# Seven half products for eight in the first layer of eleven pairs

## The chip, the cores and the metric

The kernel runs on one core of a Trainium2 chip. The metric is the device time of one execution in microseconds. Times are the median of three runs; one further execution was recorded by the hardware profiler.

## The reference

Attention with a decay (32 heads of 576 positions, head size 64) gives 2304 tokens of width 512. Two layers of the same shape follow, all in fp32:

```
x = attention(q, k, v, f)                 # 2304 x 512
h = x @ w_in;  g = relu(h)**2             # w_in: 512 x 2048
x = g @ w_out                             # w_out: 2048 x 512
h = x @ w_in2                             # second set of weights, same shapes
g = where(h >= 1, h, where(h <= -1, 0, (h + 1)**2 / 4))
out = g @ w_out2
```

Every fp32 operand of a matmul is kept as a high part (fp32r) and a low part, and each product is three matmuls: high by high, high by low, low by high.

## The kernel before

Tokens are kept as columns, in four blocks: three of 512 and a last one of 768 (`HALF` is 384). Blocks one to three run through each of the two layers pair by pair of steps: step `s` is one slice of 128 hidden units. `h_group` (L1119) makes its first layer with 12 matmuls, `act_group` (L1137) the activation and its two parts, `out_group` (L1167) adds 12 matmuls to four PSUM banks, two steps later (`LAG`). The weights of a step lie in a buffer `whl` of the ring `big` (L464, six buffers), loaded from the copy `scr` in DRAM by `w_load` (L1004). In it lie the first layer's slice of step `s + LAG` and the second layer's of step `s`. The attention of the block that follows is spread over both passes of a block: that of block three over block two, that of the last over block three. Each of its tasks sends its probabilities through transposing transfers (L930) before PE multiplies them with v (L954).

The last block is `last_block` (L1255). For each of the two layers' sets (`mo` 0 and 1, called the first and the second half here), eight pairs `c` of slices run in a first phase. A pair's first layer is four results (slice `j` by token half `k`), each 12 matmuls of 384 columns (L1333) in a PSUM bank of kind `h`; the ring `ps` has four banks, of which two hold the sums `b` (L471). ACT and DVE apply the activation and write a slot of `G` (L1344 to L1357). The second layer is done with seven half products per pair for eight already: `split` (L1274) makes high and low parts of a slot or a difference of slots, and `product` (L1287) adds 2 x 3 matmuls to two banks, which makes one half product. Three of a pair's products (`a`, `c`, `b`) stand in the first phase; the other four run in two later phases. The sums of w_out that they need are made by `weight_sums` (L1233) during the first phase: two adds 512 wide, four adds or differences 256 wide, then high and low part of each half. The first half goes to the products at once (`sum`), the other to DRAM (`scr2`), for the phase after.

Two loads bring a pair's weights from DRAM: `wi`, 1 MB in two transfers, and `wo`, the same, each into one `big` buffer. All transfers but one are issued from SP's queue.

Every operation is handed to a planner (`Schedule`, L153 on) with a due time, its costs on the engines that may do it, its dependencies and its buffers. The planner picks engine and order; the order of each engine is then fixed in the program. Rings marked fifo give their buffers out in the order in which they are made.

Of the kernel before, what the change touches and what calls it, by code (L numbers as in the profile page):

```python
# [22 lines left out]
P = 128  # L23
# [4 lines left out]
LAG = 2  # L28
# [366 lines left out]
HALF = WIDTH[LAST] // 2  # L395
NPAIR = NFC // 2
EARLY = 2


@with_exitstack  # L400
def tile_attention_moe_moe(ctx: ExitStack, tc: tile.TileContext, qkv, f, w2, outT):
# [831 lines left out]
    def weight_sums(i, due, W, o_w):  # L1233
# [18 lines left out]
        sum_op[i] = load(due + 12, lambda: Wf.tile, lambda: scr2[i], P * 4096, done[1:], [Wf], 2.0)  # L1252
        return Sb, done[0]

    def last_block():  # L1255

        n, A, v = HALF, nc.scalar, nc.vector
        x, x2 = xb[LAST], None
        t_h, t_p = 12 * mm_t(n), 6 * mm_t(n)
        t_a = 4 * t_h + 3 * t_p  # L1260
        span_mo = NPAIR * (4 * t_h + 7 * t_p)
        x2_ops = {}

        for mo in range(2):
            T0 = V[NS] + 4 * mm_t(512) + mo * span_mo
# [37 lines left out]
                return [last[key, i] for i in range(2)]  # L1303

            for c in range(NPAIR):
                tA = T0 + c * t_a
                nm = f"{mo}_{c}"
                W0, W1 = new("big", f"wi{nm}"), new("big", f"wo{nm}")
                o_w0, i = [], mo * NPAIR + c
                for j in range(2):  # L1310
                    pr = mo * NFC + (2 * c + j - LAG) % NFC
                    o_w0.append(load(tA - 8, lambda pr=pr: scr[pr][:, 0], lambda W0=W0, j=j: W0.tile[:, j].bitcast(F32),
                                     P * 4096, [scr_op[pr, 0]], [W0]))
# [5 lines left out]
                Sb, o_sb = weight_sums(i, tA, W1, o_w1)  # L1319
                gb = new("G", f"G{nm}")  # L1320
                G.append(gb)
                slots = {(0, 0): 0, (0, 1): 1, (1, 0): 2, (1, 1): 3}
                order = [(j, k) for k in (range(2) if mo == 0 else (1, 0)) for j in range(2)]
                src = x if mo == 0 else x2
                og = {}
                for at, (j, k) in enumerate(order):
                    t0 = tA + at * t_h
                    ps = new("ps", f"h{nm}_{j}{k}", kind="h")
                    o = None
                    for kc in range(NKC):  # L1330
# [12 lines left out]
                    if mo == 0:
# [16 lines left out]
                slot = lambda q, gb=gb: (lambda: gb.tile[:, q, :])  # L1360
                sp1 = split(f"1_{nm}", tA + t_h + 1.5, gb, 0, [og[0, 0]], True)
# [13 lines left out]
            tB = T0 + NPAIR * t_a + 2  # L1375
# [49 lines left out]
            for q in range(NPAIR // 2):  # L1425
                t0 = tB + 4 * q * t_p
                sb = new("big", f"s34_{mo}_{q}", [P, 2, 2, 2, 256])
                for j in range(2):
                    c = 2 * q + j
                    o_l = load(t0 - 7, lambda q=mo * NPAIR + c: scr2[q], lambda sb=sb, j=j: sb.tile[:, j].bitcast(F32),  # L1430
                               P * 4096, [sum_op[mo * NPAIR + c]], [sb])
# [122 lines left out]
```

## Time and profile before

| | us |
|---|---|
| three runs | 923.92, 925.12, 925.60 |
| median | 925.12 |
| profiled execution | 924.2 |
| its span, first to last instruction | 922.4 |
| PE busy | 913.6 |
| DVE busy | 750.7 |
| ACT busy | 688.6 |

The span has these stages: attention of block one up to about 30 us, blocks one to three up to 661, the last block's first half up to about 796 (its first phase ends near 759), and its second half to the end. PE is busy nearly throughout. The granted clock of PE is 0.999 of full speed. A busy time is the time that instructions were recorded, from first start to last end; the records of two instructions of one engine can overlap.

### The profile page before, as it was taken

The numbers are of one execution on the slowest core, as the hardware profiler recorded it, in microseconds if no ns is written. First come the engines' busy times: TensorE is split into PE (matmuls) and PEld (weight loads), VectorE is DVE, ScalarE is ACT, GpSimd is POOL, SyncE is SP. The second block draws the span as 40 slices with busy tenths as digits, with TensorE's granted clock in tenths as the row PEclk, the third lists the DMA queues.
The fourth block names the chain that finished last, engine by engine and source line by source line (L and its number), as shares of the span: only waits on it lengthen the run. The fifth ranks groups of instructions, "written<-read, shape, count | busy, mean of one in ns | idle before, by whom it ended". The sixth has DMA issues, their size and how long they took to land.

```text
span 922.4 us, 14271 instructions
## 1 busy us (share of the span) xinstructions
PE 913.6 (99%) x4674; PEld 798.8 (87%) x4674; DVE 750.7 (81%) x1738; ACT 688.6 (75%) x1375; POOL 30.6 (3%) x129
## 2 busy tenths in 40 slices
PE   8999999999999999999999999999999999999998
PEld 7678888887888888888888888888899999999998
DVE  8999999999868788887677778888677647899774
ACT  7998988999877787888778777886556555646553
POOL 4010001000000000000000000000000000000000
PEclk9999999999999999999999999999999999999999
DMA  8799999998998886989798897986687657676562
GB/s 230 246 355 399 353 402 323 363 344 323 329 297 254 249 281 205 329 226 278 234 290 278 270 267 210 277 224 179 203 289 267 222 197 279 238 264 229 213 228 86
DMA packets 132954, 247.38 MB, mean 268 GB/s; under 512 B 90513, under 2 KB 92721, under 8 KB 118097
## 3 DMA queue, kind: packets, MB, share of 16 engines
q1 hardware_dynamic: 132872, 246.47, 81.8%
q8 instruction: 37, 0.61, 0.3%
q14 instruction: 37, 0.29, 0.1%
q10 hardware_dynamic: 8, 0.00, 0.0%
HBM read 178.62 MB, written 46.84 MB: 244 GB/s over the span
## 4 chain that ended last, share of the span: by engine, by line
PE 90%; DVE 5%; ACT 2%; DMA 1%; POOL 1%; issue 1%; DVEq 0%; POOLq 0%; ACTq 0%
PE h L1129 27%; PE h L1333 13%; PE acc L1180 9%; PE acc L1182 9%; PE acc L1181 9%; PE av L954 4%; PE s L847 2%; PE s L848 2%; PE b L1296 2%; PE b L1298 2%; PE b L1297 2%; PE c L1296 1%; PE c L1298 1%; PE c L1297 1%; PE a L1297 1%; PE a L1298 1%
## 5 line engine op out<-in xcount | busy, mean ns | idle before, releaser
L1129 PE MATMUL h<-x,whl 128*128 128x512 f32 x1128 | 284.1, 393 | 0.0
L1129 PEld LDWEIGHTS h<-x,whl 128*128 128x128 f32 x1128 | 209.6, 188 | 42.5 <-issue 0.5
L1180 PE MATMUL acc<-gh,whl 128*128 128x512 f32 x384 | 150.6, 392 | 0.0
L1182 PE MATMUL acc<-gl,whl 128*128 128x512 f32 x384 | 150.1, 391 | 0.0
L1181 PE MATMUL acc<-gh,whl 128*128 128x512 f32 x384 | 149.9, 390 | 0.0
L1182 PEld LDWEIGHTS acc<-gl,whl 128*128 128x128 f32 x384 | 72.0, 188 | 15.6
L1180 PEld LDWEIGHTS acc<-gh,whl 128*128 128x128 f32 x384 | 72.1, 188 | 14.5 <-issue 0.9
L1181 PEld LDWEIGHTS acc<-gh,whl 128*128 128x128 f32 x384 | 72.1, 188 | 13.8
L881 ACT ACTIVATE E<-E,st 64x320 f32<-64x320 f32 (+2 forms) x96 | 63.4, 661 | 24.8 <-DVE st L642 19.5
L635 DVE TENSOR_TENSOR gl<-g,gh 128x512 fp32r<-128x512 f32 x96 | 65.9, 686 | 16.5 <-PE acc L1182 10.7
L642 DVE CUSTOM_DVE_ANT_0 E<-s,mask 128x288 f32<-128x288 f32 (+2 forms) x128 | 59.8, 500 | 20.6 <-PE s L848 20.2
L923 DVE SCALAR_TENSOR_TENSOR PP<-E,st,PP 128x512 f16<-128x512 f32 (+2 forms) x128 | 69.9, 592 | 5.2 <-ACT PP L919 4.3
L1333 PE MATMUL h<-x,wi 128*128 128x384 f32 x384 | 71.9, 334 | 0.0
L1333 PE MATMUL h<-x_last,wi 128*128 128x384 f32 x384 | 71.1, 336 | 0.2 <-DVE G L1357 0.2
L919 ACT ACTIVATE PP<-E,st 128x512 f16<-128x512 f32 (+2 forms) x128 | 66.9, 590 | 5.9 <-DVE st L893 4.5
L1333 PEld LDWEIGHTS h<-x_last,wi 128*128 128x128 f32 x384 | 66.8, 188 | 1.1 <-DVE G L1357 0.7
L1333 PEld LDWEIGHTS h<-x,wi 128*128 128x128 f32 x384 | 67.1, 188 | 0.4
L1227 DVE TENSOR_TENSOR G<-G 128x384 f32<-128x384 f32 x64 | 34.4, 554 | 18.7 <-ACT G L1349 18.0
L626 DVE CAST pr<-PT 128x640 fp32r<-128x640 f16 (+2 forms) x88 | 31.2, 405 | 21.7 <-DMA PT<-PP 21.7
L1160 DVE SCALAR_TENSOR_TENSOR g<-r,h 128x512 f32<-128x512 f32 x48 | 32.8, 683 | 15.5 <-ACT r L1158 14.9
L623 ACT ACTIVATE pr<-PT 128x640 fp32r<-128x640 f16 (+2 forms) x72 | 37.9, 580 | 10.0 <-DMA PT<-PP 8.8
L1156 ACT ACTIVATE r<-h,half 128x512 f32<-128x512 f32 x48 | 32.6, 679 | 16.1 <-PE h L1129 16.0
(340 smaller groups left out, 1791.6 us busy)
## 6 DMA issues: line engine op xcount, KB each, us to landing
whl<-scr SPq DMA_DIRECT2D x56, 1024.0 KB
raw<-in_w_dram SPq DMA_DIRECT2D x28, 1024.0 KB
scr<-whl SPq DMA_DIRECT2D x28, 1024.0 KB
wo<-scr SPq DMA_DIRECT2D x48, 512.0 KB
in<-in_qkv_dram SPq DMA_DIRECT2D x32, 608.0 KB
wi<-scr SPq DMA_DIRECT2D x32, 512.0 KB
whl<-scr SPq DMA_DIRECT2D x16, 512.0 KB
sum<-wfs SPq DMA_DIRECT2D x16, 512.0 KB
```

The lines of the kernel that those rows point to most:

```text
L623: alts["ACT"] = (act_t(n, psum), lambda: nc.scalar.activation(out(), in_(), AF.Copy))
L635: alts["DVE"] = (dve_t(n), lambda: nc.vector.tensor_sub(out(), a(), b()), True)
L642: return nc.vector.tensor_tensor_reduce(out=out, in0=ps, in1=mask[:m, OFF - q0:OFF - q0 + n], scale=scale, scalar=3e38, op0=ALU.add, op1=A ...
L881: nc.scalar.activation(Ec.tile[:m, :e], Ec.tile[:m, :e], AF.Exp, scale=-1.0, bias=nmx(), accum_out=st.tile[:m, 1, ci:ci + 1])))}, [*tops, ...
L919: nc.scalar.activation(hi, x, AF.Copy, scale=r())
L923: nc.vector.scalar_tensor_tensor(lo, x, r(), hi, op0=ALU.mult, op1=ALU.subtract)
L954: nc.tensor.matmul(av.tile[:, c0:W], vt.tile[:, kc, :, :], dst()[:, i, :], start=(j == 0), stop=(j == len(parts) - 1))
L1129: nc.tensor.matmul(ps.tile[:, :n], w.tile[:, 0, wi, kc * P:(kc + 1) * P], src.tile[:, kc, xi, :n], start=(kc == 0 and i == 0), stop=(kc == ...
L1180: nc.tensor.matmul(a.tile[:, :n], wh, gh.tile[:, :n], start=(fc == 0), stop=False)
L1181: nc.tensor.matmul(a.tile[:, :n], wl, gh.tile[:, :n], start=False, stop=False)
L1182: nc.tensor.matmul(a.tile[:, :n], wh, gl.tile[:, :n], start=False, stop=(fc == NFC - 1))
L1333: nc.tensor.matmul(ps.tile[:, :n], W0.tile[:, j, wi, kc * P:(kc + 1) * P], src.tile[:, kc, xi, k * n:(k + 1) * n], start=(kc == 0 and i == ...
```

## The change

In the last block, pairs 2 to 7 of the first half and 3 to 7 of the second (`SEVEN`) make their first layer with seven half products of six matmuls each, on two PSUM banks, in place of four results of 12. The function `seven` does it. It needs sums of w_in (four per pair) and sums of the tokens. The token sums are made once per half by `token_sums`, on DVE and ACT, due while pair 0 runs; their parts are kept in `xa` and in buffers of `o` and `g`, which the last block doesn't use otherwise at that time. The sums of w_in are made in block three by `pair_sums`, in the pass over the same weights, from the `whl` buffers of two steps, and stored in DRAM (`scr3`, high and low part, 0.5 MB each); `seven` loads them into a third `big` buffer per pair. Of `wi` such a pair loads only three of four quarters.

For pairs 3 to 6 of the second half (`OUTS`) the sums of w_out come the same way from block two (`scr4`); for these `weight_sums` is not called.

The core of the diff:

```diff
+SEVEN = ((2, 3, 4, 5, 6, 7), (3, 4, 5, 6, 7))
+SUMS_AT = (2, 2)
+OUTS = ((), ((1, 3), (1, 4), (1, 5), (1, 6)))
...
+    def in_sums(s):
+        blk, mo, fc = steps[s]
+        c = fc // 2
+        if fc % 2 == 0:
+            if blk == SUMS_AT[mo] and c in SEVEN[mo]:
+                pair_sums(s, s - LAG, 0, scr3[mo, c], in_sum_op)
+            if (blk, c) in OUTS[mo]:
+                pair_sums(s, s, 1, scr4[mo, c], out_sum_op)
+
+    def pair_sums(s, first, layer, store, ops):
...
+        due = V[s + 1] + 2 * layer
+        Wf, Sf, Sh = new("wf", f"wfi{nm}"), new("low", f"si{nm}", [P, 4, 256], F32), new("wf", f"shi{nm}")
+        for j in range(2):
+            w, o_w = whl[first + j], whl_op[first + j]
+            o_f.append(add(due + j, lambda j=j: Wf.tile[:, j], lambda w=w: w.tile[:, layer, 0].bitcast(F32),
+                           lambda w=w: w.tile[:, layer, 1].bitcast(F32), 512, o_w, [w, Wf]))
...
+        o1 = add(due + 2, S[0], A21, A22, 256, o_f[1:], [Wf, Sf])
+        o2 = add(due + 2.5, S[1], S[0], A11, 256, [o1, o_f[0]], [Wf, Sf], sub=True)
+        o3 = add(due + 3, S[2], A11, A21, 256, o_f, [Wf, Sf], sub=True)
+        o4 = add(due + 3.5, S[3], A12, S[1], 256, [o2], [Wf, Sf], sub=True)
+        o5 = sch.op(due + 4, copies(lambda: flat(Sh), src, 1024, "ACT DVE"), [o3, o4], [Sf, Sh])
+        o6 = sch.op(due + 5, subs(lambda: flat(Wf), src, lambda: flat(Sh).bitcast(F32), 1024, "DVE"), [o5], [Sf, Sh, Wf])
+        ops[mo, c] = [load(due + 10 + i, ..., P * 4096, [o], [b], 2.0) for i, b, o in ((0, Sh, o5), (1, Wf, o6))]
...
+        def token_sums(due, mo, x, x_ops):
...
+            for kk in range(2):
+                xf, tf = new("G", f"xf{mo}{kk}"), new("G", f"tf{mo}{kk}")
+                o_x = [add(due + kk * 6, lambda q=q, whole=whole: whole(q), lambda q=q, kk=kk: x.tile[:, 2 * q + kk, 0].bitcast(F32),
+                           lambda q=q, kk=kk: x.tile[:, 2 * q + kk, 1].bitcast(F32), 2 * n, x_ops(2 * q + kk), [x, xf])
+                       for q in range(2)]
+                o1 = add(due + kk * 6 + 1, T[0], B12, B11, n, o_x[:1], [xf, tf], sub=True)
+                o2 = add(due + kk * 6 + 1.5, T[1], B22, T[0], n, [o1, o_x[1]], [xf, tf], sub=True)
+                o3 = add(due + kk * 6 + 2, T[2], B22, B12, n, o_x, [xf, tf], sub=True)
+                o4 = add(due + kk * 6 + 2.5, T[3], B21, T[1], n, [o2], [xf, tf], sub=True)
+                for t, o in enumerate((o1, o2, o3, o4)):
+                    o = sch.op(due + kk * 6 + 3, copies(hi, T[t], n, "ACT DVE"), [o], [tf, hb])
+                    o = sch.op(due + kk * 6 + 4, subs(lo, T[t], lambda hi=hi: hi().bitcast(F32), n, "DVE"), [o], [tf, hb, lb])
+
+        def seven(mo, c, tA, W0, o_w0, gb, x, x_ops):
+            sb = new("big", f"si{nm}")
+            o_s = [load(tA - 6, ... scr3[mo, c][:, i] ..., P * 4096, [in_sum_op[mo, c][i]], [sb]) for i in range(2)]
+            X, Y = (new("ps", f"{z}{nm}", kind="h") for z in "XY")
+            c_ = [new("C", f"c{i}{nm}") for i in range(3)]
+            p, q, v_ = ((lambda b=b: b.tile) for b in c_)
...
+            m1 = mul(0, X, A_(0, 0), B_(0, 0), True, [], c_)
+            o_p = sch.op(tA + t_p, copies(p, xs, n, "ACT DVE", psum=True), [m1], [X, c_[0]])
+            m6 = mul(1, Y, S_(1), T_(1), True, [])
+            o_q = plus(2, q, ys, p, [m6, o_p], [Y, c_[0], c_[1]])
+            m2 = mul(2, X, A_(0, 1), B_(1, 0), False, [m1, o_p])
+            g11 = act(3, xs, 0, m2, X, True)
+            m7 = mul(3, Y, S_(2), T_(2), False, [m6, o_q])
+            o_v = plus(4, v_, ys, p, [m7, o_p], [Y, c_[0], c_[2]])
+            m5 = mul(4, X, S_(0), T_(0), True, [m2, g11])
+            o_22 = plus(5, v_, xs, v_, [m5, o_v], [X, c_[2]])
+            m4 = mul(5, Y, A_(1, 1), T_(3), False, [m7, o_v])
+            o_21 = plus(6, p, ys, p, [m4, o_q, o_v], [Y, c_[0]])
+            m3 = mul(6, X, S_(3), B_(1, 1), False, [m5, o_22])
+            o_12 = plus(7, q, xs, q, [m3, o_q], [X, c_[1]])
+            return {(0, 0): g11, (1, 1): act(5.5, v_, 3, o_22, c_[2]), (1, 0): act(6.5, p, 2, o_21, c_[0]),
+                    (0, 1): act(7.5, q, 1, o_12, c_[1])}
...
+                    z = 256 if c in SEVEN[mo] and j else 0
+                    o_w0.append(load(tA - 8, ... scr[pr][:, 0, :, z:] ..., P * 8 * (512 - z), [scr_op[pr, 0]], [W0]))
...
+                if (mo, c) in scr4:
+                    Sb = new("sum", f"sum{nm}")
+                    o_sb = load(tA + t_a - 7 * t_p, ... scr4[mo, c][:, :, :2] ..., P * 4096, out_sum_op[mo, c], [Sb])
+                else:
+                    Sb, o_sb = weight_sums(i, tA, W1, o_w1)
...
+                if c in SEVEN[mo]:
+                    og = seven(mo, c, tA, W0, o_w0, gb, src, x_ops)
+                if c == 0 and SEVEN[mo]:
+                    token_sums(tA + 4, mo, src, x_ops)
-                for at, (j, k) in enumerate(order):
+                for at, (j, k) in enumerate(() if og else order):
...
             w_decode(s + 1)
+            in_sums(s)
```

In `act`, the first result (`g11`) is read from its bank; where the second half's activation or the first half's `g11` needs it, ACT writes `r` first. The other three results are read from SBUF.

## Rows read from the trace of the kernel before

**Rows 1.** The page: part 1, then the first line of part 4.

```profile
PE 913.6 (99%) x4674; PEld 798.8 (87%) x4674; DVE 750.7 (81%) x1738; ACT 688.6 (75%) x1375; POOL 30.6 (3%) x129
...
PE 90%; DVE 5%; ACT 2%; DMA 1%; POOL 1%; issue 1%; DVEq 0%; POOLq 0%; ACTq 0%
```

**Rows 2.** Busy times by stretch; the first row names the columns.

```profile
core 0: us, PE busy (x) PEld busy (x) DVE busy (x) ACT busy (x) POOL busy (x), PEclk, DMA share, GB/s
30.00:140.00 110.00, 109.93 (x538) 87.42 (x537) 108.44 (x203) 101.23 (x179) 7.51 (x3) 1.00 0.96 358
350.00:455.00 105.00, 105.00 (x512) 89.01 (x511) 87.37 (x232) 83.01 (x174) 1.76 (x19) 1.00 0.83 253
455.00:555.00 100.00, 100.00 (x489) 84.74 (x488) 74.68 (x203) 78.85 (x170) 2.20 (x24) 1.00 0.88 269
555.00:660.00 105.00, 104.86 (x504) 88.31 (x503) 84.69 (x211) 78.55 (x162) 1.87 (x18) 1.00 0.82 224
685.00:708.00 23.00, 23.00 (x135) 23.00 (x134) 16.50 (x33) 13.02 (x26) 0.00 (x0) 1.00 0.89 299
812.00:830.00 18.00, 17.80 (x102) 17.48 (x102) 17.10 (x36) 9.65 (x18) 0.00 (x0) 1.00 0.72 259
830.00:853.00 23.00, 23.00 (x134) 22.78 (x133) 21.09 (x42) 14.14 (x26) 0.00 (x0) 1.00 0.64 229
```

**Rows 3.** Timeline of PE, 690 to 730: start, us, engine, line, operation, tiles, count.

```profile
704.45 3.80 PE L1333 MATMUL h<-x,wi 128*128 128x384 f32 x21
...
715.89 3.80 PE L1333 MATMUL h<-x,wi 128*128 128x384 f32 x21
```

**Rows 4.** Timeline of all engines, 880 to 890: two banks handed over; [idle before <-releaser].

```profile
881.89 0.33 PE L1298 MATMUL a<-gl,wo 128*128 128x384 f32 x1
...
882.28 1.00 ACT L623 ACTIVATE p<-a 128x384 f32<-128x384 f32 x2
...
882.81 0.19 PEld L1296 LDWEIGHTS a<-ghaB,wo 128*128 128x128 f32 x1 [0.39 <-ACT p L623]
...
885.35 0.33 PE L1298 MATMUL c<-ghl,sum 128*128 128x384 f32 x1
...
885.72 1.08 DVE L1227 TENSOR_TENSOR w<-c,p 128x384 f32<-128x384 f32 x2
...
886.33 0.19 PEld L1296 LDWEIGHTS c<-ghlcB,s 128*128 128x128 f32 x1 [0.45 <-DVE w L1227]
```

**Rows 5.** Timeline of DVE, 700 to 730, the same columns.

```profile
699.93 0.42 DVE L1227 TENSOR_TENSOR sf<-wfs 128x256 f32<-128x256 f32 x1
700.39 0.42 DVE L1227 TENSOR_TENSOR sf<-sf,wfs 128x256 f32<-128x256 f32 x1
...
702.80 0.69 DVE L635 TENSOR_TENSOR wfs<-sf,wfs 128x512 fp32r<-128x512 f32 x1
703.41 0.55 DVE L635 TENSOR_TENSOR gl<-G,gh 128x384 fp32r<-128x384 f32 x1
...
713.66 1.02 DVE L1227 TENSOR_TENSOR G<-G 128x384 f32<-128x384 f32 x2
```

**Rows 6.** Timelines, one activation in each half: ACT from 705.69, all from 800.22.

```profile
705.69 0.49 ACT L1344 ACTIVATE r<-h 128x384 f32<-128x384 f32 x1 [0.41 <-PE h L1333]
706.22 0.53 ACT L1349 ACTIVATE G<-r 128x384 f32<-128x384 f32 x1
...
800.22 0.58 ACT L1352 ACTIVATE r<-h,half 128x384 f32<-128x384 f32 x1 [1.94 <-PE h L1333]
...
801.39 0.55 DVE L1357 SCALAR_TENSOR_TENSOR G<-r,h 128x384 f32<-128x384 f32 x1 [2.20 <-ACT r L1354]
```

**Rows 7.** SP's own waits, 662 to 760: who waited for whom, us, times, longest.

```profile
SPq L1223 <- PE a L1298: 51.2, 9, 9.5
```

**Rows 8.** Waits of all engines, 447 to 661, the same columns.

```profile
DVE pr L626 <- DMA PT<-PP: 11.9, 10, 1.9
```

More of the change, by code (lines that the diff above doesn't have):

```diff
@@ L1253, in weight_sums @@
         return Sb, done[0]
+    scr3 = {(mo, c): dram.tile([P, 2, 4, 256], F32, name=f"in_sum{mo}_{c}") for mo in range(2) for c in SEVEN[mo]}
+    scr4 = {(mo, c): dram.tile([P, 2, 4, 256], F32, name=f"out_sum{mo}_{c}") for mo in range(2) for _, c in OUTS[mo]}
+    in_sum_op, out_sum_op = {}, {}
+    def in_sums(s):
[7 more added lines that the diff above has]
+    def pair_sums(s, first, layer, store, ops):
+        blk, mo, fc = steps[s]
+        c = fc // 2
+        nm = f"{layer}_{mo}_{c}"
+        due = V[s + 1] + 2 * layer
+        Wf, Sf, Sh = new("wf", f"wfi{nm}"), new("low", f"si{nm}", [P, 4, 256], F32), new("wf", f"shi{nm}")
+        o_f = []
+        for j in range(2):
+            w, o_w = whl[first + j], whl_op[first + j]
+            o_f.append(add(due + j, lambda j=j: Wf.tile[:, j], lambda w=w: w.tile[:, layer, 0].bitcast(F32),
+                           lambda w=w: w.tile[:, layer, 1].bitcast(F32), 512, o_w, [w, Wf]))
+        (A11, A12), (A21, A22) = ([lambda j=j, z=z: Wf.tile[:, j, z:z + 256] for z in (0, 256)] for j in range(2))
+        if layer:
+            A12, A21 = A21, A12
+        S = [lambda i=i: Sf.tile[:, i] for i in range(4)]
+        o1 = add(due + 2, S[0], A21, A22, 256, o_f[1:], [Wf, Sf])
+        o2 = add(due + 2.5, S[1], S[0], A11, 256, [o1, o_f[0]], [Wf, Sf], sub=True)
+        o3 = add(due + 3, S[2], A11, A21, 256, o_f, [Wf, Sf], sub=True)
+        o4 = add(due + 3.5, S[3], A12, S[1], 256, [o2], [Wf, Sf], sub=True)
+        src = lambda: Sf.tile.rearrange("p a n -> p (a n)")
+        flat = lambda b: b.tile.rearrange("p a n -> p (a n)").bitcast(F32R)
+        o5 = sch.op(due + 4, copies(lambda: flat(Sh), src, 1024, "ACT DVE"), [o3, o4], [Sf, Sh])
+        o6 = sch.op(due + 5, subs(lambda: flat(Wf), src, lambda: flat(Sh).bitcast(F32), 1024, "DVE"), [o5], [Sf, Sh, Wf])
+        ops[mo, c] = [load(due + 10 + i, lambda b=b: b.tile.rearrange("p a n -> p (a n)"),
+                             lambda i=i: store[:, i].rearrange("p a n -> p (a n)"), P * 4096, [o], [b], 2.0)
+                        for i, b, o in ((0, Sh, o5), (1, Wf, o6))]
     def last_block():
@@ new lines, in seven, with A_, S_, B_ @@
+        def seven(mo, c, tA, W0, o_w0, gb, x, x_ops):
+            nm = f"7{mo}_{c}"
+            sb = new("big", f"si{nm}")
+            o_s = [load(tA - 6, lambda i=i: scr3[mo, c][:, i].rearrange("p a n -> p (a n)"),
+                        lambda i=i: sb.tile[:, i].rearrange("p a n -> p (a n)").bitcast(F32), P * 4096, [in_sum_op[mo, c][i]], [sb])
+                   for i in range(2)]
+            X, Y = (new("ps", f"{z}{nm}", kind="h") for z in "XY")
+            c_ = [new("C", f"c{i}{nm}") for i in range(3)]
+            p, q, v_ = ((lambda b=b: b.tile) for b in c_)
+            xs, ys = lambda: X.tile[:, :n], lambda: Y.tile[:, :n]
+            def A_(j, k):
+                return W0, [o_w0[j]], lambda i, kk: W0.tile[:, j, i, 256 * k + P * kk:256 * k + P * kk + P]
+            def S_(i):
+                return sb, o_s, lambda h, kk: sb.tile[:, h, i // 2, 256 * (i % 2) + P * kk:256 * (i % 2) + P * kk + P]
+            def B_(k, t):
+                return [x], [o for kk in range(2) for o in x_ops(2 * k + kk)], lambda i, kk: x.tile[:, 2 * k + kk, i, t * n:(t + 1) * n]
+            def T_(t):
+                return ([b for kk in range(2) for b in tsum[mo, t, kk][1]], [tsum[mo, t, kk][2] for kk in range(2)],
+                        lambda i, kk: tsum[mo, t, kk][0][i]())
+            def mul(at, bank, a, b, start, deps, extra=()):
+                (wb, wo, wt), (bs, bo, bt) = a, b
+                def mms():
+                    todo = [(kk, wi, xi) for kk in range(2) for wi, xi in ((0, 0), (0, 1), (1, 0))]
+                    for z, (kk, wi, xi) in enumerate(todo):
+                        nc.tensor.matmul(bank.tile[:, :n], wt(wi, kk), bt(xi, kk), start=start and z == 0,
+                                         stop=z == len(todo) - 1, skip_group_check=not start)
+                return sch.op(tA + at * t_p, {"PE": (6 * mm_t(n), mms)}, [*deps, *wo, *bo],
+                              list(dict.fromkeys([bank, wb, *bs, *extra])), mlp=True)
+            plus = lambda at, out, a, b, deps, bufs: add(tA + at * t_p, out, a, b, n, deps, bufs, psum=True)
+            def act(at, src, slot, dep, buf, bank=False):
+                out, due = lambda: gb.tile[:, slot, :], tA + at * t_p
+                r = None if mo == 0 and not bank else new("r", f"r{nm}_{slot}")
+                rt = lambda: r.tile[:, :n]
+                def on_act():
+                    A.activation(src(), src(), AF.Relu)
+                    A.activation(out(), src(), AF.Square)
+                port = () if bank else (True,)
+                if r is None:
+                    return sch.op(due, {
+                        "DVE": (dve_t(n), lambda: v.scalar_tensor_tensor(out(), src(), 0.0, src(), op0=ALU.max, op1=ALU.mult), True),
+                        "ACT": (2 * act_t(n), on_act)}, [dep], [buf, gb])
+                if mo == 0:
+                    o = sch.op(due, {"ACT": (act_t(n, True), lambda: A.activation(rt(), src(), AF.Relu))}, [dep], [buf, r])
+                    return sch.op(due + 0.5, {
+                        "DVE": (dve_t(n), lambda: v.scalar_tensor_tensor(out(), src(), 0.0, rt(), op0=ALU.max, op1=ALU.mult)),
+                        "ACT": (act_t(n), lambda: A.activation(out(), rt(), AF.Square))}, [o], [buf, r, gb])
+                def squared():
+                    A.activation(rt(), src(), AF.Relu, scale=0.5, bias=half)
+                    A.activation(rt(), rt(), AF.Square)
+                o = sch.op(due, {"ACT": (act_t(n, True, 1) + act_t(n), squared)}, [dep], [buf, r])
+                return sch.op(due + 1, {"DVE": (dve_t(n), lambda: v.scalar_tensor_tensor(
+                    out(), rt(), 1.0, src(), op0=ALU.min, op1=ALU.max), *port)}, [o], [buf, r, gb])
+            m1 = mul(0, X, A_(0, 0), B_(0, 0), True, [], c_)
[14 more added lines that the diff above has]
+                    (0, 1): act(7.5, q, 1, o_12, c_[1])}
@@ L1305, in last_block @@
             for c in range(NPAIR):
-                tA = T0 + c * t_a
+                tA = T0 + starts[mo][c]
                 nm = f"{mo}_{c}"
@@ L1311, in last_block @@
                     pr = mo * NFC + (2 * c + j - LAG) % NFC
[L1312 to L1313 removed]
+                    z = 256 if c in SEVEN[mo] and j else 0
+                    o_w0.append(load(tA - 8, lambda pr=pr, z=z: scr[pr][:, 0, :, z:], lambda W0=W0, j=j, z=z: W0.tile[:, j, :, z:].bitcast(F32),
+                                     P * 8 * (512 - z), [scr_op[pr, 0]], [W0]))
                 o_w1 = []
@@ L1318, in last_block @@
                                      P * 4096, [scr_op[pr, 1]], [W1]))
-                Sb, o_sb = weight_sums(i, tA, W1, o_w1)
+                if (mo, c) in scr4:
+                    Sb = new("sum", f"sum{nm}")
+                    o_sb = load(tA + t_a - 7 * t_p, lambda c=c: scr4[mo, c][:, :, :2].rearrange("p t a n -> p t (a n)"),
+                                lambda Sb=Sb: Sb.tile.bitcast(F32), P * 4096, out_sum_op[mo, c], [Sb])
+                else:
+                    Sb, o_sb = weight_sums(i, tA, W1, o_w1)
                 gb = new("G", f"G{nm}")
@@ L1325, in last_block @@
                 og = {}
-                for at, (j, k) in enumerate(order):
+                x_ops = lambda kc: xops[LAST, kc] if mo == 0 else [x2_ops[kc, k] for k in range(2)]
+                if c in SEVEN[mo]:
[3 more added lines that the diff above has]
+                for at, (j, k) in enumerate(() if og else order):
                     t0 = tA + at * t_h
@@ L1360, in last_block @@
                 slot = lambda q, gb=gb: (lambda: gb.tile[:, q, :])
+                te -= t_p * (c in SEVEN[mo])
                 sp1 = split(f"1_{nm}", tA + t_h + 1.5, gb, 0, [og[0, 0]], True)
@@ L1374, in last_block @@
                              [o_sb], sp6, first, stop)
-            tB = T0 + NPAIR * t_a + 2
+            tB = T0 + starts[mo][NPAIR] + 2
             o_u, o_w = [], []
@@ L1429, in last_block @@
                     c = 2 * q + j
-                    o_l = load(t0 - 7, lambda q=mo * NPAIR + c: scr2[q], lambda sb=sb, j=j: sb.tile[:, j].bitcast(F32),
-                               P * 4096, [sum_op[mo * NPAIR + c]], [sb])
+                    done = (mo, c) in scr4
+                    part = scr4[mo, c][:, :, 2:].rearrange("p t a n -> p t (a n)") if done else scr2[mo * NPAIR + c]
+                    o_l = load(t0 - 7, lambda part=part: part, lambda sb=sb, j=j: sb.tile[:, j].rearrange("p t a n -> p t (a n)").bitcast(F32),
+                               P * 4096, out_sum_op[mo, c] if done else [sum_op[mo * NPAIR + c]], [sb])
                     for z, key, slot, dep, e in ((1, "c", 3, "b22", 0), (0, "b", 1, "t3", 1)):
```

16 lines of the change are left out of this document (15 added, 1 removed).

## The prediction

> **What bounds the kernel now.** I read the page first: TensorE (PE) is busy 913.6 of 922.4 us, and 90% of the chain that ended last is PE [rows 1]. That is an average, so next comes the table of stretches, where the reader should look at the PE and the VectorE (DVE) columns side by side [rows 2]. PE is full nearly throughout: 105.00 of 105.00 us in block two's second pass, 100.00 of 100 and 104.86 of 105 in block three, 23.00 of 23.00 in the last block's first half. The largest share that it misses in these rows is 0.20 us of the 18 from 812 to 830, where DVE is at 17.10. So in the last block a PE instruction taken away is worth its own time, as long as nothing else reaches 100%. DVE is the candidate: 16.50 of 23 us in the first half of the last block, 21.09 of 23 in the second, 75 to 83% in blocks two and three. What a busy DVE can do without stopping PE is seen from 30 to 140 us: DVE 108.44 of 110, and PE 109.93.
>
> **What is removed.** Now a pair's first layer is eight half products of six matmuls, and its second layer adds three more in the first phase. The timeline of PE gives the step of one matmul: 21 take 3.80 us, the last one shown to its end, so (3.80 - 0.33)/20 = 0.1735 us [rows 3, 4]; a half product is 6 x 0.1735 = 1.04 us, and 11 of them are 11.44, which is also the distance from one pair to the next (715.89 - 704.45) [rows 3]. Eleven pairs lose one half product each: 11 x 1.04 = 11.4 us of PE that is on the path. Such a pair then lasts 10.40 us.
>
> Four pairs of the second half also lose their weight sums: two adds 512 wide, four 256 wide, two differences 512 wide. By starts in the timeline of DVE, 512 wide is 0.61 us (702.80 to 703.41), 256 wide behind its own result 0.46 (699.93 to 700.39), 384 wide 0.47 (two in 1.02, one taking 0.55) [rows 5]: 4 x 0.61 + 4 x 0.46 = 4.3 us of DVE a pair. PE gets nothing from that directly; it pays for what follows.
>
> **What is added in the last block.** A seven-product pair runs on two PSUM banks in turn. Each product waits until the bank's last product has been dealt with, and one other product (1.04 us) lies between. Five of these steps are adds on DVE from PSUM that are not there today. I price them by the add of the same kind that exists, w<-c,p, two in 1.08 us, so 0.47 to 0.55 each [rows 4]: 5 x 0.47 = 2.35 us. The pair's DVE work in the first half is then 4.3 (weight sums) + 4 x 0.47 (G adds) + 3 x 0.47 (splits) + 2.35 = 9.9 us of 10.40; in the second half four activations come on top and, in four of the five pairs, the weight sums go: 4 x 0.47 + 3.3 + 2.35 = 7.5. DVE fits, barely in the first half. ACT gets one copy more a pair and the squares of g11, some 0.5 to 1 us, and has 13.02 of 23 us in use [rows 2].
>
> Does the hand-over fit under the 1.04 us? One place shows it bare, where a phase of the last block ends: the last matmul into a starts at 881.89, ACT copies at 882.28, the next matmul into that bank loads at 882.81, after 0.39 us of idle; by DVE 885.35, 885.72, 886.33, with 0.45 idle [rows 4]. From the last matmul's start that is 0.92 and 0.98 us, so 0.75 and 0.81 after it is issued: 0.23 to 0.29 us to spare, if the engine is free at that moment. One step is longer. The first result of each pair is squared straight from its bank. In the first half that is two ACT steps, 0.53 apart, the second 0.53 long [rows 6]: 0.39 + 1.06 + 0.04 - 0.17 = 1.32 after issue, 0.28 too long. In the second half it is two ACT steps and one on DVE, 801.39 + 0.55 - 800.22 = 1.72 [rows 6], which makes 0.39 + 1.72 + 0.06 - 0.17 = 2.00, 0.96 too long. Over six and five pairs: 6 x 0.28 + 5 x 0.96 = 6.5 us at most, and 0 at least, since each pair has three second-layer products (3.12 us) that wait for none of this and can stand there. I take a quarter, **1.6**, as one uncovered wait of today (0.39 less the 0.17 of a matmul) is about a quarter of 0.96.
>
> The other six hand-overs of a pair, 66 in all, cost nothing if DVE is free, and up to 0.47 - 0.23 = 0.24 us each behind another add: 0 to 15.8, the far end being a DVE that never is free (A, below). I take **1.0**, near zero, because from 812 to 830 a DVE at 95% took only 0.20 us from PE in 18 [rows 2].
>
> Token sums: once in each half, 4 adds 768 wide (no row; between one and two 384-wide ones, I take 2 x 0.47), 8 differences and 8 low parts at 0.47: 11.3 us of DVE, while pairs 0 and 1 (first half) or 0 to 2 (second) still run the old way. Old pairs need 4.3 + 3.3 = 7.6 there and 9.5 here, so 26.5 us fall due in 22.9 and 39.8 in 34.3: a debt of 3.6 and 5.5. Later pairs pay back 6 x 0.5 = 3.0 and 4 x 2.9. Cost 0 to 9.1; I take **1.7**: the unpaid 0.6 of the first half and a fifth of the second's.
>
> Loads. A pair now fetches 0.79 + 1.05 + 1.05 MB and stores or fetches 0.52 more, 3.4 MB in 10.40 us, 328 GB/s; today's best stretch has 299 at a share of 0.89, which is 336 at 1 [rows 2]. Three instead of two of the six big buffers go to a pair, so the sync queue (SP), which already waits 51.2 us for products to free a buffer [rows 7], has loads of pair c+2 queued behind the end of pair c. I count nothing: each has a whole pair's time to land. Its price, if not, is a rival below.
>
> **What is added in blocks two and three.** Fifteen sums of pairs: each 4.3 - 2 x 0.61 of adds as above, one copy on either engine, one difference 1024 wide (no row; at most 2 x 0.61): some 4.3 us of DVE and two stores of 0.52 MB. Four fall in 350 to 455, six in 455 to 555, five in 555 to 660: DVE 87.4 + 17 = 104 of 105, 74.7 + 26 = 101 of 100, 84.7 + 22 = 106 of 105 by recorded durations, some 87% of that by starts (0.47 for 0.55, 0.61 for 0.69) [rows 2, 5]. Transfers: 6.3 MB in 455 to 555 are 63 GB/s or, at 358 GB/s for a share of 0.96 [rows 2], 0.17 on top of 0.88: 1.05, some 5 us too many, with 0.14 on 0.82 behind it. Queued behind each store on SP are the transposes of the attention, for which DVE's casts already wait 11.9 us [rows 8], and behind those the last block's tokens. PE has other work (two steps of second-layer products) ready when they are late. Bounds 0 and 5; I take **0.5**.
>
> The sum: the profiled execution took 924.2 us (span 922.4 and 1.8 around it); 924.2 - 11.4 + 1.6 + 1.0 + 1.7 + 0.5 = 917.6. The median of the three timed runs, 925.12, is 0.9 above that execution, so the forecast is **918.5**.
>
> **Rivals.** (A) DVE becomes the bound of the last block, and the kernel is slower. This is so if an instruction holds DVE for its recorded duration and not for the distance of starts. Then a pair of the first half has 16.50/2.01 = 8.2 + 5 x 0.55 = 11.0 us, and the half 2 x 8.2 + 12.8 + 6 x 11.0 = 95 (12.8 being the token sums, 4 x 1.0 + 16 x 0.55). The second half has 3 x 10.5 + 12.8 + 4 x 8.8 + 13.3 = 93: 10.5 is 21.09/2.01, 8.8 is that less 4 x 0.69 + 4 x 0.42 of weight sums and with 5 x 0.55 more, 13.3 the last pair, which keeps them [rows 2, 5]; together 188 against today's 16 x 11.44 = 183: **930**. The sign turns once DVE's sum passes those 183. Against it: two adds of 0.55 start 0.47 apart [rows 5]; for it: adds that need the one before start later than the record's 0.42 [rows 5]. The Trainium skill has such a rule, in "VectorE: DVE Perf Modes", section "The DRAIN you can't avoid": the next instruction doesn't start until the pipe is empty. By that rule (A) would hold; the trace does not agree where two adds have no tie, 0.47 against 0.55.
>
> (B) Transfers bound the seven-product pairs: at the 299 GB/s of today's best stretch 3.4 MB take 11.4 us, the old pair: the gain is gone, **924 to 925**; under 299 it is slower. Against: 358 GB/s from 30 to 140 [rows 2].
>
> (C) The stage before slips: the 5 us of transfers and DVE's 101 to 106% move the last tokens, and PE runs out of other work: 918.5 + 4 = **922.5**.
>
> (D) All waits are covered: 925.1 - 11.4 = **913.7**.
>
> **How the numbers follow.** Forecast (914 to 921.5) 0.62, A 0.12, B 0.09, C 0.10, D 0.07. From 914.0, nearly all of D's gain, to 925.0, B's end, leaves out A and half of D, under 2 in 10. A measurement of this kernel can tell about 0.2%, 1.9 us, from no change. Faster (below 923.3): forecast, D and nearly all of C, 0.78; within: B less its tails and the rest of C, 0.09; slower: A and a tail of B, 0.13.
>
> **What would show it.** Right: pairs 2 to 7 of the first half and 3 to 7 of the second about 10.5 us apart, PE over 97% busy there, DVE 90% or more, the last block still starting near 661 us. Wrong: that start moved (C); DVE without a gap and PE waiting for v, q or p (A), or for T at the first seven-product pair (token sums); PE waiting for si or wi (B); PE waiting for G at each fifth product by more than 0.3 us (the quarter was too little). A span 11 us shorter would say that the waits cost nothing.

## The result and the profile after

The changed kernel takes 929.75 us, the median of 18 runs (926.15 to 932.70); 18 runs of the kernel before on the same chips took 924.38 (923.68 to 926.88). The ratio is 1.0052, with a 95% interval of 1.0042 to 1.0062: **slower by half a per cent**, where 918.5 was forecast and 925.0 was the end of the range. The profiled execution took 926.75, one of the shorter ones, over a span of 924.9.

Busy times and the first line of the chain of waits of the changed kernel, to be set beside [rows 1]:

```profile
PE 907.9 (98%) x4608; PEld 785.6 (85%) x4608; DVE 828.3 (90%) x1898; ACT 706.2 (76%) x1413; POOL 29.1 (3%) x128
...
PE 69%; DVE 17%; ACT 5%; DMA 5%; issue 2%; POOL 1%; SPq 0%; ACTq 0%; DVEq 0%; POOLq 0%
```

PE has 66 matmuls fewer (4674 - 4608), 11 half products of six: that part is as announced. But the chain of waits is 69% PE instead of 90%; DVE (17% for 5), ACT (5 for 2) and DMA (5 for 1) took most of the rest. Where? The stretches of [rows 2], of the changed kernel (PE busy with its count, weight loads, DVE, ACT, POOL, clock, DMA share, GB/s):

```profile
350.00:455.00 105.00, 102.40 (x496) 85.78 (x495) 96.03 (x249) 83.32 (x174) 1.76 (x19) 1.00 0.96 283
455.00:555.00 100.00, 98.45 (x471) 81.81 (x470) 91.87 (x226) 84.33 (x179) 2.21 (x24) 1.00 1.01 309
555.00:660.00 105.00, 103.43 (x499) 86.55 (x498) 95.69 (x241) 82.86 (x173) 1.87 (x18) 1.00 0.93 275
660.00:760.00 100.00, 99.26 (x549) 95.08 (x548) 94.78 (x195) 58.60 (x117) 0.00 (x0) 1.00 0.91 298
```

PE has gaps before the last block even begins. From 350 to 660 the matmuls are 496 + 471 + 499 = 1466; [rows 2] has 512 + 489 + 504 = 1505. The 39 that are missing, at 105/512 = 0.205 us each, are 8.0 us of work put off. (The busy time shows only 309.86 - 304.28 = 5.6 of it: a matmul's record lasts longer than the step to the next matmul, and a short gap hides in it. Counts in equal stretches are the safer reading.) The last block's first product appears just as much later; the first weight loads of tile `h`, before and after (first to last start):

```profile
L1333 PEld LDWEIGHTS h<-x,wi x384: 187/188/188, 661.2 to 756.1; 128*128 128x128 f32 x192
```
```profile
L1505 PEld LDWEIGHTS h<-x,wi x96: 187/188/188, 669.8 to 694.3; 128*128 128x128 f32 x96
```

It starts 8.6 us late, and from there to the end takes 924.9 - 669.8 = 255.1 us instead of 922.4 - 661.2 = 261.2. So the last block did gain 6.1, and blocks two and three lost 8.6. What PE waited for there, and who waited for tile `PT`, the transposed probabilities (us, times, longest; us, times):

```profile
PE av L957 <- ACT pr L626: 2.3, 3, 0.9
PE h L1132 <- ACT r L1161: 1.7, 1, 1.7
...
  PEld av L957: 4.7, 6
```

In the kernel before the list for `PT` has no line of PE's. Of PE's waits in the changed kernel, 5.6 us in all, only 2.6 are directly for the casts `pr`, and DVE and ACT together wait for `PT` no longer than before, 17.7 us against 17.8. The chain in order of time and PE's timeline show one of these waits:

```profile
402.17 0.53 DVE E L645
402.69 6.18 DMA PT<-PP
...
408.97 1.36 ACT pr L626 x2
```
```profile
409.76 1.49 PE L957 MATMUL av<-pr,vt 128*128 128x320 f32 x9 [0.92 <-ACT pr L626]
416.37 3.01 PE L1132 MATMUL h<-x,whl 128*128 128x512 f32 x12 [1.68 <-ACT r L1161]
```

The last of three transposes took 6.18 us from the start of its issue to its landing, ACT's cast `pr` came after that, and the attention's product stood at the head of PE's order, which left PE idle for 0.92 us with all other work behind that product. ACT had stood still for 2.46 us before the cast; from there it worked without a gap up to the activation `r` that PE waited for next, so the same delay reached PE a second time, as 1.68 us. SP itself needed longer to issue the three, 7.63 us; the next three of the kernel before took 4.00 (SP's queue, after, then before):

```profile
397.89 7.63 SPq L933 DMA_TRANSPOSE PT<-PP  x3
```
```profile
408.25 4.00 SPq L930 DMA_TRANSPOSE PT<-PP  x3
```

### The profile page after: what moved, and what is told of

It is laid out like the page before. It is cut to its first block, busy times and chain, and to the rows that moved or that the text cites. A ratio compares the mean times of both kernels' runs of the same rounds, so it can differ in the third digit from the quotient of the medians.

```text
span 924.9 us, 14449 instructions
## 1 busy us (share of the span) xinstructions
PE 907.9 (98%) x4608; PEld 785.6 (85%) x4608; DVE 828.3 (90%) x1898; ACT 706.2 (76%) x1413; POOL 29.1 (3%) x128
## 4 chain that ended last, share of the span: by engine, by line
PE 69%; DVE 17%; ACT 5%; DMA 5%; issue 2%; POOL 1%; SPq 0%; ACTq 0%; DVEq 0%; POOLq 0%
PE h L1132 22%; PE acc L1183 7%; PE acc L1185 7%; PE acc L1184 7%; PE h L1505 4%; PE X L1371 3%; PE av L957 3%; PE Y L1371 2%; DMA PT<-PP 2%; PE b L1457 2%; PE b L1458 2%; PE b L1459 2%; PE s L850 2%; PE s L851 2%; DVE PP L926 1%
## 5 line engine op out<-in xcount | busy, mean ns | idle before, releaser
L626 ACT ACTIVATE pr<-PT 128x640 fp32r<-128x640 f16 (+2 forms) x74 | 40.1, 595 | 11.6 <-DMA PT<-PP 11.5
L957 PE MATMUL av<-pr,vt 128*128 128x320 f32 (+2 forms) x288 | 45.3, 300 | 2.7 <-ACT pr L626 2.3
L957 PEld LDWEIGHTS av<-pr,vt 128*128 128x128 f32 x288 | 41.4, 189 | 7.3 <-ACT pr L626 4.3
L629 DVE CAST pr<-PT 128x640 fp32r<-128x640 f16 (+2 forms) x86 | 30.0, 395 | 17.7 <-DMA PT<-PP 16.6
L850 PE MATMUL s<-K,Q 128*128 128x288 f32 (+2 forms) x128 | 39.6, 320 | 0.3 <-DVE st L645 0.3
L851 PE MATMUL s<-K,Q 128*128 128x288 f32 (+2 forms) x128 | 39.6, 317 | 0.0
L1109 DVE SCALAR_TENSOR_TENSOR whl<-wf,whl 128x1024 fp32r<-128x1024 f32 (+1 forms) x32 | 37.9, 1186 | 0.1
```

The lines of the kernel that those rows point to most:

```text
L850: nc.tensor.matmul(out, q2[:, q0:q0 + m], k2[:, s0:s1], start=True, stop=False)
L851: nc.tensor.matmul(out, Q1.tile[:, q0:q0 + m], K1.tile[:, s0:s1], start=False, stop=True)
L957: nc.tensor.matmul(av.tile[:, c0:W], vt.tile[:, kc, :, :], dst()[:, i, :], start=(j == 0), stop=(j == len(parts) - 1))
```

## The experiments

The theory after the result: the attention of the next block, with its transposes, is delayed by what the sums put into blocks two and three, and PE, whose order is fixed, stands still for it. It leaves open whether DVE's work or the stores do it. The rival: the last block is at fault (DVE bound, or loads). Runs e1 to e4 shared a chip with the kernel before at 925.00, e5 to e8 at 924.71, e9 to e11 at 924.56; across these groups compare ratios.

**e1, the last block alone.** No sums are made; the loads of sums read slices of the weights instead.

```diff
-            in_sums(s)
-  ... scr3[mo, c][:, i] ...
+  ... scr[mo * NFC + (2 * c + i - LAG) % NFC][:, 0] ...
```

> Leaves out the sums in blocks two and three; the last block runs its seven products on slices of the weights in place of the sums, so that only its time counts. Between the traces the last block starts 8.5 us later (669.9 against 661.4) and takes 6.0 us less (255.0 against 261.0). Theory T (transfers of blocks two and three) and theory D (DVE there) both expect the last block's own gain alone: about 924.4 - 6 = 918.5. Theory L, that the last block doesn't gain by itself, expects 924 or more.

**917.32 us**, ratio 0.9926 [0.9909, 0.9942]. The last block starts where it did, and is 914.9 - 660.9 = 254.0 long, 7.2 shorter than before. Its first stretch, and tile `h`:

```profile
660.00:760.00 100.00, 99.88 (x564) 97.35 (x564) 95.36 (x196) 55.92 (x115) 0.00 (x0) 1.00 0.89 302
```
```profile
L1505 PEld LDWEIGHTS h<-x,wi x96: 187/188/188, 660.9 to 687.2; 128*128 128x128 f32 x96
```

DVE at 95.36 of 100 by its records, and PE at 99.88: neither DVE nor the loads bound the last block in this stretch.

**e2, the sums alone.** They are made and stored; the last block runs as before.

```diff
     def last_block():
+        SEVEN, scr4 = ((), ()), {}
```

> The sums of blocks two and three are made and stored, and the last block runs as in the kernel before and doesn't use them. T and D: the 8.5 us of the later start of the last block, with nothing given back: 924.4 + 8.5 = 933, or up to 936 as the timed runs of the changed kernel lie 3 us above its profiled one. L: 925 to 926.

**938.18 us**, 1.0143 [1.0121, 1.0166]: the sums cost 13.2 us, and the time is 2 us above the most that was expected. With the 7.7 of e1 the two halves of the change make 5.5, and the whole change costs 929.75 - 924.38 = 5.4. They add up, so what is left to find is on the sums alone, which cost 7.7 + 5.4 = 13.1 in the whole change.

**e3, sums without stores; e4, stores without sums.** e3 has the last block of e1, e4 that of the changed kernel, which loads what was stored. In e4 POOL fills the buffers with ones, and the same 30 stores of 0.52 MB go out.

```diff
 e3
-        ops[mo, c] = [load(due + 10 + i, ..., P * 4096, [o], [b], 2.0) for i, b, o in ...]
 e4
-            o_f.append(add(due + j, lambda j=j: Wf.tile[:, j], ...
-        o1 ... o6
+        o5, o6 = (sch.op(due + 4 + i, {"POOL": (1.0, lambda b=b: nc.gpsimd.memset(b.tile, 1.0))}, ...) ...)
```

> The sums are made on DVE and ACT but not stored; the last block fetches slices of the weights in their place, of the same size. T: the stage before is free again, 918.5 to 920, start of the last block near 662. D: the loss stays, 928 to 930, start near 669.

> No sums are made; the same number of bytes is stored at the same due times from buffers that GpSimd fills with ones, and the last block runs on those. T: the loss stays, 927 to 930, start of the last block near 669. D: 918.5 to 920, start near 662. If both e3 and e4 lose about half, both loads count.

e3 **921.52** (0.9963 [0.9948, 0.9978]), e4 **930.26** (1.0070 [1.0044, 1.0097]). e3 falls between its two expectations, e4 just above T's. Over e1 the adds cost 4.2 us and the stores, with POOL's fills, 12.9; both together 13.1, so the delays are shared and don't add. The same three stretches, first e3, then e4:

```profile
350.00:455.00 105.00, 103.88 (x504) 87.45 (x503) 95.05 (x240) 85.32 (x179) 1.94 (x21) 1.00 0.83 255
455.00:555.00 100.00, 99.76 (x484) 84.17 (x484) 95.49 (x247) 87.87 (x185) 2.05 (x22) 1.00 0.91 265
555.00:660.00 105.00, 104.15 (x503) 87.67 (x502) 99.91 (x247) 84.42 (x170) 1.88 (x18) 1.00 0.76 214
```
```profile
350.00:455.00 105.00, 102.94 (x498) 86.29 (x497) 84.83 (x223) 82.35 (x174) 9.29 (x27) 1.00 0.97 292
455.00:555.00 100.00, 97.37 (x467) 81.19 (x466) 71.06 (x192) 76.16 (x161) 13.34 (x36) 1.00 1.06 306
555.00:660.00 105.00, 100.87 (x481) 83.62 (x480) 81.78 (x212) 77.24 (x162) 11.06 (x28) 1.00 0.95 273
```

e3 has the busiest DVE and the emptier transfers, e4 a DVE with less to do than before and the full ones; e4's PE lacks 1505 - 1446 = 59 matmuls, e3's 14. Who waited for `PT` in e4, and PE's longest wait:

```profile
  DVE pr L629: 36.3, 16
  ACT pr L626: 26.8, 17
  PEld av L957: 8.2, 8
```
```profile
PE av L957 <- ACT pr L626: 4.2, 5, 1.4
```

DVE and ACT wait for the transposes 63.1 us, 17.8 in the kernel before and 4.8 in e3. With the stores the transposes come late.

**e5, an eighth of the bytes.** As the full change to the sums, with all 30 stores in their places, 128 columns each. **e6, loads for stores.** As e4, with loads of the same size from the weights' copy in place of the stores and of POOL's fills. Both have the last block of e1.

```diff
 e5
-  b.tile ... store[:, i] ...            P * 4096
+  b.tile ...[:, :128], store[:, i] ...[:, :128], P * 512
 e6
-  o5, o6 = memsets;  store <- b.tile
+  b.tile <- scr[mo * NFC + (2 * c + i - LAG) % NFC][:, 0]
```

> As e3, the sums made and the last block on slices of the weights, but with all 30 stores issued at their places, each with an eighth of its bytes (128 of 1024 columns). Theory T1, the bytes fill the transfer engines: an eighth of the 13 us that e4 lost against e1, on top of e3's 921.5: 922 to 924. Theory T2, it is the extra places in SP's queue, which hold up the transposes behind them whatever their size: 928 to 931.

> As e4, no sums made, but each store is replaced by a load of the same 0.52 MB from DRAM into the same buffer. T1: reads or writes, the bytes count: 928 to 932, as e4's 930.3. Theory T3, writes to DRAM are what holds the transposes up: 917 to 921.

e5 **923.83** (0.9990 [0.9981, 1.0000]), 2.5 us by ratio over e3, where the stores with all their bytes cost 8.2 (the whole change over e3): most of the price goes with the bytes. What the 30 places in SP's queue cost by themselves the intervals can't tell. e6 **925.68** (1.0008 [0.9996, 1.0020]): the same bytes as loads cost 0.0082 of the time over e1, some 7.6 us, where the stores cost 0.0144, 13.3. That lies between T1 and T3: more than half of the price is that of any transfers of these bytes, not of stores alone. DVE and ACT wait for the transposes 61.1 us in e6, about as long as in e4, and only 0.2 in e5: full-sized copies in either direction make the transposes late, the same number of small ones doesn't. What the stores cost beyond that may be the writing or POOL's fills, which e6 doesn't have (POOL is busy for 33.7 us in e4's three stretches, for 5.8 in [rows 2]).

**e7, the first half's sums only; e8, the same spread over two blocks.** Six pairs in the first half, the second half as before, no sums of w_out. In e7 all six sums are made in block three's pass, in e8 those of even `c` in block two and those of odd `c` in block three. Both compute the whole reference.

```diff
+SEVEN = ((2, 3, 4, 5, 6, 7), ())
+OUTS = ((), ())
 e8 only
-            if blk == SUMS_AT[mo] and c in SEVEN[mo]:
+            if blk == 1 + c % 2 and c in SEVEN[mo]:
```

> Seven half products in the first half of the last block alone (six pairs), no sums of w_out from block two; all six sums of w_in in block three's first pass. The first half's own gain in e1 is 127.9 - 122.5 = 5.4 us. If each pair's sums and stores cost the mean of e1, e3 and e4, (13.0 + 4.2)/15 = 1.15 us: 925.0 - 5.4 + 6.9 = 926.5. If only what goes over the room of a pass costs: also 925 to 927, since all six fall in the fullest pass.

> As e7, with the six sums spread: three in block two's first pass and three in block three's. If each pair costs its mean: 926.5 as e7. If only what goes over the room of a pass costs (share 0.90 to 0.94 and 0.88 to 0.91 before, 0.08 more each): 921 to 923.

e7 **924.75** (0.9997 [0.9988, 1.0007]), e8 **921.94** (0.9964 [0.9952, 0.9977]). The same adds and bytes, 0.3% apart. e8's stretches:

```profile
245.00:350.00 105.00, 104.97 (x508) 88.63 (x507) 91.87 (x237) 82.86 (x174) 2.38 (x26) 1.00 1.01 309
350.00:455.00 105.00, 105.00 (x512) 89.02 (x511) 87.01 (x232) 83.06 (x175) 1.76 (x19) 1.00 0.86 257
455.00:555.00 100.00, 100.00 (x489) 84.65 (x488) 84.34 (x222) 82.25 (x174) 2.21 (x24) 1.00 1.04 297
```

PE loses next to nothing, and the last block starts at 660.3, though two stretches have shares of 1.01 and 1.04. (This profiled execution, 918.93, is the shortest of e8's seven.) e7's middle rows are 1.08 for 455 to 555 and 0.82 for 555 to 660, and PE's busy time is 99.53 of 100 and 103.36 of 105: the larger loss comes in the stretch behind the full one.

```profile
455.00:555.00 100.00, 99.53 (x479) 83.40 (x478) 89.70 (x228) 83.53 (x175) 2.04 (x22) 1.00 1.08 309
555.00:660.00 105.00, 103.36 (x498) 86.63 (x498) 85.49 (x221) 80.93 (x166) 1.88 (x18) 1.00 0.82 234
```

So a loss can come a pass after the full one. What carries it there is not shown: PE's list of waits in e7 has none for the casts `pr` (the weight loads wait 0.5 us for them), and its longest is for DVE's part of an activation:

```profile
PE s L850 <- DVE g L1163: 1.0, 1, 1.0
```

Both the adds and the bytes are spread in e8, so the pair doesn't tell which of them the 2.8 us between e7 and e8 belong to.

**e9, e1 without the token sums.** The products read the tokens themselves.

```diff
-                if c == 0 and SEVEN[mo]:
-                    token_sums(tA + 4, mo, src, x_ops)
```

> As e1 (last block alone on slices of the weights), and without the token sums: the products that use them read the tokens themselves. My step put the token sums at 1.7 us: 917.3 - 1.7 = 915.6. Rival: later work takes up the DVE debt and PE never waits for it: 917.3 within 0.6, and the loss of 3.7 us in the last block lies in the hand-overs and the ends of the phases.

**918.96 us**, 0.9946 [0.9929, 0.9962], not faster than e1's 0.9926: the 1.7 us put down for the token sums isn't there. It is some 1.8 us slower by ratio, more than the 0.6 that was expected; three of its four executions ran at a mean granted clock of 0.996 to 0.998.

**e10, five pairs; e11, half the bytes.** e10 is e8 with pairs 3 to 7. e11 is e10 with each sum stored once, 0.52 MB a pair, and split into high and low part in the last block.

```diff
 e10
+SEVEN = ((3, 4, 5, 6, 7), ())
 e11
-        o5 = sch.op(due + 4, copies(lambda: flat(Sh), ...
-        o6 = sch.op(due + 5, subs(lambda: flat(Wf), ...
+        ops[mo, c] = load(due + 8, ... Sf.tile ... store ..., P * 4096, [o3, o4], [Sf], 2.0)
```

> As e8, with five pairs of the first half in place of six: two sums in block two, three in block three. The last block's own gain 5 x 0.9 = 4.5. If a pair's sums cost the mean of e8, (5.4 - 2.8)/6 = 0.43: 924.7 - 4.5 + 2.2 = 922.4. If only the fullest moments cost, less: 921.

> As e10, with half the bytes: a sum is stored as it is (0.52 MB a pair) and split into high and low part in the last block after the load, in place. If bytes cost and DVE holds (its first half by starts 89.6 us of 92): 920.5 to 921.5, under e10. If DVE becomes the bound of the first half (1.2 us more a pair, not hidden): 923 to 927, over e10.

e10 **921.38** (0.9969 [0.9958, 0.9980]), e11 **921.22** (0.9964 [0.9951, 0.9977]). With the sums spread, neither one pair fewer nor half the bytes moves the median by what the intervals can tell. The scatter may change: 920.90 to 921.54 in e11's five runs, 919.96 to 923.81 in e10's ten. e8, e10 and e11 beat both kernels, the one before by 0.31 to 0.36%.

## Why the prediction was wrong, step by step

**The failing step is the term of 0.5 us for blocks two and three**, with 5 as its upper end. It measured 13.1 (13.2 in e2), against 4 for rival C, whose mechanism it is in the main: C had PE run out of other work, while in the trace PE has work left, but behind the product that it waits for. Forecast was a change of 918.5 - 925.1 = -6.6, measured +5.4, 12.0 apart: 12.6 of it this term, less the 0.6 by which the last block came out better than forecast.

The share itself was well estimated: 1.05 was worked out for 455 to 555, 1.01 was recorded, and 1.06 in e4. What failed is how it was turned into time. *First*, only the excess over 1 in a mean over 100 us was priced. The loss of the pass from 350 to 455, with a mean of 0.96, is 105 - 102.40 = 2.60 us of PE, and all of it falls in 20 us:

```profile
400.00:420.00 20.00, 17.40 (x82) 14.04 (x81) 17.44 (x44) 14.85 (x33) 0.28 (x3) 1.00 1.17 303
```

*Second*, the transposes were named as queued behind the stores, and then counted as covered by two steps of second-layer products. That cover is real: before the change one stretch of 20 us with a share of 1.12 costs PE nothing:

```profile
240.00:260.00 20.00, 20.00 (x98) 16.88 (x97) 13.10 (x37) 15.81 (x36) 0.55 (x6) 1.00 1.12 278
```

But it is not there every time: at 409.76 and 416.37 the next product in PE's fixed order was not ready. That a late task makes the next one late, and that three passes in a row at 0.93 to 1.01 leave no slack to win it back, is argued and not shown: e8, with 0.86 behind its 1.01, fits it, but e7 loses its time with 0.82 behind its 1.08. *Third*, DVE's 101 to 106% was named and priced at nothing by itself. Its records came to 91 or 92% of the three stretches; e3, at 91 to 95%, still loses 4.2 us.

**Removed, 11.4: right.** 66 matmuls, and one pair of the first half to the next, by the same product of each in e1's timeline of PE:

```profile
697.91 1.20 PE L1371 MATMUL X<-x,wi 128*128 128x384 f32 x6
...
708.34 1.20 PE L1371 MATMUL X<-x,wi 128*128 128x384 f32 x6
```

10.43 us, 10.40 forecast, 11.44 before [rows 3].

**The last block's costs, 1.6 + 1.0 + 1.7 = 4.3: the sum right, its parts not.** e1 gains 7.7 of 11.4, so 3.7 are lost. Of these the token sums are nothing (e9). The waits for g11 are 0.3, and the other hand-overs 2.0 as waits of the weight loads, where 1.0 was taken; the same list shows si, rival B's transfer, at 0.5 (e1, from 660 to 915: us, times, longest):

```profile
PEld Y L1371 <- DVE c L1230: 1.2, 3, 0.6
PEld X L1371 <- ACT c L626: 0.8, 2, 0.5
...
PEld Y L1371 <- DMA si<-scr: 0.5, 2, 0.3
...
PEld X L1371 <- DVE G L1405: 0.3, 1, 0.3
```

One cost was not in the sum: where the second half's first phase ends. The last pair's seven products end in adds and activations of `c`, and PE has nothing else left (e1, timeline of PE):

```profile
875.28 0.34 PE L1459 MATMUL a<-glaB,wo 128*128 128x384 f32 x1
876.55 0.44 PE L1457 MATMUL c<-ghl,sum 128*128 128x384 f32 x1 [0.93 <-ACT ghl L626]
...
878.47 0.44 PE L1457 MATMUL c<-ghlcB,s 128*128 128x384 f32 x1 [0.36 <-DVE w L1230]
...
879.22 0.34 PE L1457 MATMUL b<-ghl,sum 128*128 128x384 f32 x1
```

Ten matmuls from 875.28 to 879.22 take 3.94 us instead of 1.74: 2.2 us. The kernel before loses 0.7 at the same place (30 matmuls from 881.54 to 887.49 take 5.95 us instead of 5.21), so 1.5 of it came with the change. That is about half of what the second half lacks: it gains 133.5 - 131.5 = 2.0 of its 5.2 us, the first half 127.7 - 122.5 = 5.2 of 6.2.

**Rival A fell.** DVE's records fill 95% of e1's stretch with PE at 99.88, and adds of 0.55 without a tie start 0.48 and 0.46 apart:

```profile
713.74 0.56 DVE L1230 TENSOR_TENSOR c<-Y,c 128x384 f32<-128x384 f32 x1
714.22 0.55 DVE L638 TENSOR_TENSOR gl<-G,gh 128x384 fp32r<-128x384 f32 x1
714.68 0.55 DVE L1230 TENSOR_TENSOR G<-G 128x384 f32<-128x384 f32 x1
```

The Trainium skill, "VectorE: DVE Perf Modes", section "The DRAIN you can't avoid", has the next operation wait until the pipe is empty, and excepts one that is not held. The prediction left the exception out; the trace agrees with it here, 0.48 and 0.46 against 0.55. **B fell**: the pair takes 10.43 us, not 11.4. **D** was not reached.

**What stays open.** The profiled execution of after is 926.75, its median 929.75; the trace explains the former. Of the 3 us between them the granted clock explains a part: the five executions with a mean clock of 0.998 or 0.996 took 929.89 to 932.70, and the other 13 have a median of 928.71. Where the other 2 us go was not seen. How much of the stores' surplus over loads is the writing itself, how much POOL's fills and how much their places among the transposes was not taken apart either, nor how much of e3's and e4's loss is the planner's other order of the same work.

## What to carry to other kernels

Work moved to where an engine has room must be priced at what shares its transfers: ask which short transfers with someone waiting behind them (here the transposes) lie between the new ones, and look at stretches of a few tasks' length, not at the mean of a pass. A cover such as two steps of spare work can be used up; count how often it is drawn on and what fills it up again. If work must move, spread it: the same six sums cost 2.8 us less over two blocks than in one.

## What the runs showed of the hardware

The busy share of the transfer engines and the bytes moved are different things here. From 400 to 420 the changed kernel moves 303 GB/s at a share of 1.17 and PE starves; in the kernel before, from 30 to 140, it was 358 GB/s at 0.96 with PE at 109.93 of 110 [rows 2]. The Trainium skill, "Perfetto Trace Analysis", section "Identifying the Most-Contended Engine", advises going by the bytes against the memory's rate rather than by occupancy, and then finding which resource of the transfers binds. By the bytes alone 303 GB/s would be the less loaded stretch, yet it is the one that lost 2.60 us. The share alone doesn't tell either, since 1.12 cost PE nothing from 240 to 260 of the kernel before.

A share above 1 over 100 us is itself something that the records show (e7: 1.08). It counts the time for which packets were open, and these times overlap: at 404.5 of the changed kernel 28 packets are open on the 16 engines. In slices of half a microsecond this can mislead. Those of 400 to 420 (share in tenths, then GB/s) look nearly empty from 403.5 to 405 and from 406.5 to 407.5, inside the 6.18 us of the wait that ends at 408.87:

```profile
DMA  9999999240999106997969997999999999999599
GB/s 479 399 425 409 348 249 104 78 71 18 226 312 209 2 10 142 445 492 295 524 262 418 467 457 286 516 393 369 393 410 483 377 426 377 351 217 51 113 245 285
```

But a packet's whole time is put into the slice in which it begins, as the stretch before the first gap shows, with its share of 2.77:

```profile
402.00:403.50 1.50, 1.50 (x9) 1.26 (x8) 1.50 (x7) 1.39 (x6) 0.00 (x0) 1.00 2.77 234
403.50:405.00 1.50, 1.50 (x10) 1.32 (x9) 1.46 (x4) 1.23 (x3) 0.00 (x0) 1.00 0.23 55
```

In the trace's packets the engines are not idle there; they hold packets of 256 bytes, the transposes' own, that stand still. The median packet of this kind takes 0.02 us; 26 that begin from 402.66 to 404.13 all end from 405.03 to 405.08, and 17 that begin from 406.35 to 406.50 end at 407.76 to 407.78. From 350 to 661 there are 156 such packets of over 0.9 us in the changed kernel, 182 in e4 and 233 in e6, but 94 in the kernel before, 75 in e3 and 70 in e5: more of them come with the full-sized copies. They don't settle the loss alone, since e8's profiled execution has 152 and PE loses next to nothing. What the packets wait for no run here shows.

A gap of PE may cost more than its own length. In e6's profiled execution PE stands for 2.95 us up to 411.43, and from 412.8 to 416.2 its granted clock is at 0.51, the lower of its two levels (1.2 and 2.4 GHz), which costs (1 - 0.51) x 3.40 = 1.7 us more:

```profile
412.80:416.20 3.40, 3.40 (x10) 2.61 (x9) 3.19 (x7) 3.05 (x9) 0.00 (x0) 0.51 1.03 391
```

In e2's profile the clock falls in the same way after gaps of 1.53 and 0.36 us; in the changed kernel's, after 0.92 us, it doesn't. Nine of e6's ten executions have a mean clock of 0.998 or less, so a part of its 7.6 us is the clock's.

Executions of the changed kernel scatter more: 926.15 to 932.70, against 923.68 to 926.88 of the kernel before. That full transfers are the reason is not shown.
